# A longer planned distance between the loads and the sums of pooled keys and values in a fused attention and feed-forward kernel

## The chip, the cores and the metric

One NeuronCore of one Trainium2 chip runs the whole kernel. The metric is the device time of one execution in microseconds (us), given as the median of the runs; lower is better. The engines of the core are TensorE (PE in the profile; PEld is its weight load), VectorE (DVE), ScalarE (ACT), GpSimd (POOL) and SyncE (SP), which only issues transfers (DMAs) here. Each engine works through its own list of instructions in order.

## The reference

Attention over keys and values that are averaged in groups of eight tokens, and a feed-forward layer with softplus behind it:

```python
B, H, S, D = 8, 8, 576, 64          # q, k, v: (B, H, S, D), float32
k_p = k.reshape(B, H, 72, 8, D).mean(axis=3)
v_p = v.reshape(B, H, 72, 8, D).mean(axis=3)
scores = matmul(q, k_p.T) / sqrt(D)
attn = exp(scores - max) ; attn = attn / (sum(attn) + 1e-9)
x = matmul(attn, v_p)               # tokens x 512: (4608, 512)
h = x @ w_in                        # (512, 2048)
g = maximum(h, 0) + log1p(exp(-abs(h)))
out = g @ w_out                     # (2048, 512) -> (4608, 512)
```

## The kernel before

The 4608 tokens are cut into 18 chunks of 256 (`NCH`, numbered c = 0 to 17). A batch b has 576 tokens, so a new batch begins every 2.25 chunks, and a chunk has rows of one batch or of two. Products that need float32 accuracy are made of three fp32r products of a high and a low part.

**Chunks.** For each chunk, attention makes scores, probabilities and x, and the feed-forward layer then runs over eight pairs of rows of `w_in` and `w_out` (u = 0 to 7): the first product (line 678, 24 matmuls, output `h`), softplus on ScalarE (lines 686 and 700), sums and low parts on VectorE (lines 737 to 740, 707, 756), and the second product. For chunks 0 to 3 that is a plain product (lines 652 and 719), from chunk 4 on (`NF`) a product in 21 matmuls over sums of blocks (line 826, output `m`). During a steady chunk c the attention of chunk c + 1 is done in between: scores (line 490), then least values, differences, exponential, sums, transposes of the probabilities (line 556, `ptp`), and the product with the values (lines 597 and 604, `avp`).

**Two lists.** The order of all instructions is planned ahead by the class `Order` (lines 37 to 99). Every piece of work is an `op` with an engine, a cost, the ops that it comes after, the buffers (`Slot`) that it holds, and a lag: the time that must pass, in the plan, between its end and the start of an op on another engine that follows it (line 74). The planner runs through time and picks for an engine, among the ops that could start soon, the one with the highest rank; a rank is the longest way from the op to the end, costs and lags added (line 55), and some ops have a bonus (`first`) on top. What comes out is only an order on each engine. On the chip an instruction waits for semaphores that follow from the tiles that it reads and writes, not for planned times. The first list covers chunks 0 to 2 and the conversion of the weights; the steady list, from line 1375 on, covers the rest. Only the steady list has an object attribute `pause` (line 1382); in the first list `todo.pause` is the empty dictionary of the class.

**Keys and values.** `keys_values(b)` (line 1213) makes the ops of one batch, for b = 2 in the first list and for b = 3 to 7 in the steady list. Inside it `pooled` (line 1223) makes a pair: a load on SyncE into one of four staging buffers (`LD`, line 154), and a sum over eight tokens on VectorE (`tree`, line 227: two instructions on the staging buffer and one that writes the pooled tile). A batch has four such pairs for keys (line 263, one DMA each), two for values (line 275, two DMAs each) and one for the last eight rows of the values (line 287, four small DMAs, called the left rows here). In the plan, the load of a pair comes after the sum of the pair two places before it. After the four sums of keys, TensorE transposes them (line 234) and ScalarE writes `kT`; after the two of values, ScalarE writes `vs` (line 244); after the left rows come lines 299 and 251 and last line 253, which writes `vlo`, on which the first load of the next batch depends in the plan. `kT`, `vs` and `vlo` have two buffers each, by b % 2.

**What stands beside them.** On SyncE: `load_wi` (line 854), two DMAs of 512 KB for each pair u from chunk 4 on, as soon as TensorE has read the rows that they overwrite; the loads of q (line 333); the stores of the output (line 664); loads and stores of combined weights (lines 800 and 807) in chunks 3 and 4. On TensorE, inside the scores of a chunk: all but the last 1/8 of them go to two PSUM banks, the last eighth twice into one place, so that VectorE must copy the first of the two out (`keep`, line 504, `E<-x`) before TensorE may write the second (line 490, `x<-kT,qT`).

Of the kernel before, what the change touches and what calls it, by code (L numbers as in the profile page):

```python
# [30 lines left out]
class Order:  # L31
# [11 lines left out]
    def op(self, engine, cost, fn, after=(), slots=(), lag=None, rest=0, first=0, table=None):  # L43
        o = Op(engine, cost, fn, after, slots, self.HOP if lag is None else lag, len(self.ops))
        o.rest, o.first, o.table = rest, first + self.first, table
        for x in o.after:
            x.followers.append(o)
        for x in slots:
            x.users.append(o)
        self.ops.append(o)  # L50
        return o
# [54 lines left out]
def pooled_attention_softplus_ffn(  # L106
# [125 lines left out]
    def k_transposes(ps, kp):  # L232
        for m in range(HP):
            nc.tensor.transpose(out=ps[:, m * SP:(m + 1) * SP],
                                in_=kp[:, 2 * m:2 * m + 2].rearrange("p h d -> p (h d)"),
                                identity=ident[0:SP, 0:SP])

    def k_scaled(b, ps):

        nc.scalar.activation(out=kT[b % 2], in_=ps[:, 0:HP * SP].rearrange("p (m y) -> p m y", m=HP),  # L240
                             func=AF.Copy, scale=SCALE)

    def v_scaled(b, vp):
        nc.scalar.activation(out=vs[b % 2], in_=vp, func=AF.Copy, scale=1.0 / POOL)

    def left_part(b, i, lt):

        R, vx = 4 * KL, vlo[b % 2]
        lv = lt.rearrange("p a (m c) d -> p (a m) (c d)", c=2)
        if i < 2:  # L250
            nc.scalar.copy(out=vx[i * R:(i + 1) * R], in_=lv)
        else:
            nc.vector.tensor_tensor(out=vx[2 * R:3 * R], in0=lv, in1=vx[0:R].bitcast(F32),
                                    op=ALU.subtract)
# [51 lines left out]
    def spans(lo, hi):  # L306

        cut = sorted({lo, hi, *(x for x in range(0, NTOK, S) if lo < x < hi)})
        return [(x, y, x // S) for x, y in zip(cut, cut[1:])]
# [5 lines left out]
    def ones():  # L315
        x = one.tile([P, T, H, SP], F32, tag="E", name="ones").rearrange("p t h y -> p (t h y)")
        nc.vector.memset(x[:, 0:512], 1.0)
        return x
# [542 lines left out]
    todo = Order(kinds)  # L861
    op = todo.op
    ACT, DVE, PE, SYNC = (nc.scalar.engine, nc.vector.engine, nc.tensor.engine, nc.sync.engine)
    todo.begin, todo.table = {SYNC: 0.8, DVE: 0.8, PE: 0.8, ACT: 2.0}, "exp"

    def bank(s, name):
        if s.tile is None:
            s.tile = psum.tile([P, 512], F32, tag=s.name, name=name)
        return s.tile
# [3 lines left out]
    def act(n):  # L873
        return 0.14 + 0.00094 * n
# [338 lines left out]
    def keys_values(b, free_k=None, free_v=None):  # L1213
        x = kv(b)
        batches = lambda c: {y for _, _, y in spans(c * CT, (c + 1) * CT)}
        s_kp, s_vp, s_lt, s_vl = Slot("kp"), Slot("vp"), Slot("kp"), Slot("vp")

        old = [c for c in range(N1 + 1, NCH) if b - 2 in batches(c)]
        free_k = free_k or [o for c in old for o in score_done.get(c, ())]
        free_v = free_v or [o for c in old for o in av_done.get(c, ())]  # L1220
        ends = [v_ready[b - 1][-1] if b > 3 else None]

        def pooled(load, pool, time, slot, after=()):

            s = Slot("ld")
            o = op(SYNC, time, lambda: load(s), ends[-2:][:1], [s], lag=2.4)
            ends.append(op(DVE, 1.4, pool, [o, *after], [s, slot]))
            return ends[-1]

        sums_ = [pooled(lambda s, i=i: x["k_load"](i, s), lambda i=i: x["k_pool"](i), 1.2, s_kp)  # L1230
                 for i in range(HP)]
        s_t = Slot("bank")
        o = op(PE, 0.3, lambda: k_transposes(bank(s_t, "kT"), x["kp"][0]), [*sums_, *free_k],
               [s_t, s_kp], first=100)
        k_ready[b] = [op(ACT, act(288), lambda: k_scaled(b, s_t.tile), [o], [s_t])]
        sums_ = [pooled(lambda s, i=i: x["v_load"](i, s), lambda i=i: x["v_pool"](i), 1.2, s_vp)
                 for i in range(2)]
        v_ready[b] = [op(ACT, act(256), lambda: v_scaled(b, x["vp"][0]), [*sums_, *free_v], [s_vp])]
        o = pooled(lambda s: x["left_load"](s), x["left"], 1.0, s_vl, v_ready[b])
        o = op(DVE, 1.1, x["lasts"], [o, *k_ready[b]], [s_vl, s_lt])  # L1240
        parts = [op(ACT, 0.65, lambda i=i: left_part(b, i, x["st"]["lt"]), [o, *free_v], [s_lt])
                 for i in range(2)]
        v_ready[b].append(op(DVE, 0.7, lambda: left_part(b, 2, x["st"]["lt"]), parts, [s_lt]))
# [21 lines left out]
    o = op(DVE, 0.3, lambda: x_w.append(ones()), first=2000)  # L1265
# [113 lines left out]
    ends = {e: max(o.end for o in todo.ops if o.engine == e) for e in (ACT, DVE, PE, SYNC)}  # L1379
    todo = Order(kinds)  # L1380
    todo.begin = {e: max(0, t - ends[PE]) for e, t in ends.items()}
    todo.pause = {PE: 0.05, DVE: 0.5}
    op = todo.op
# [293 lines left out]
```

## Time and profile before

| | |
|---|---|
| median of 3 runs | 896.26 us (895.38 to 896.85) |
| the profiled execution | 896.75 us |
| its span, first to last instruction | 895.0 us |
| TensorE busy in the span | 873.6 us (98%) |
| VectorE, ScalarE busy | 643.9 us (72%), 418.1 us (47%) |
| mean granted TensorE clock | 0.989 of full speed |

The span is what the trace covers; 1.75 us of the execution lie around it. A share of busy time is a mean over stages, so what a single place costs is read from the waits and from stretches of the timeline. A releaser named beside an idle time is the event that came last ahead of the waiting instruction.

### The profile page before, as it was taken

The page shows a single profiled execution, that of the slowest core. Times are in us where ns is not written, and L with a number is a line of the kernel's source. Part 1 is how long each engine was busy: PE and PEld are TensorE (multiplying, and loading weights), DVE is VectorE, ACT ScalarE, POOL GpSimd, SP SyncE. Part 2 cuts the span into 40 slices and gives each one's busy share as a digit, 9 for nine tenths or more (in the row PEclk, how much of TensorE's full clock was granted, in tenths as well). Part 3 has the DMA queues.
Part 4 walks back from the last instruction along what each step waited for, and adds up shares of the span by engine and source line. Part 5 has one row for each costly group of instructions (what it writes and reads, how often), then busy time and mean ns, then how long its engine had stood idle before and what let it go on. Part 6 is the DMA issues. An engine that isn't in the chain of part 4 may idle for free.

```text
span 895.0 us, 20398 instructions
## 1 busy us (share of the span) xinstructions
PE 873.6 (98%) x8280; PEld 831.0 (93%) x8280; DVE 643.9 (72%) x1531; ACT 418.1 (47%) x851; POOL 2.4 (0%) x19
## 2 busy tenths in 40 slices
PE   6899999999999999998999999999999999999997
PEld 3688989888999999998999899999999999999997
DVE  6899998888867788685667756787676565656454
ACT  5854343355463636452554445353636353525332
POOL 1000000000000000000000000000000000000000
PEclk8999999999999999998999999999999999999999
DMA  8964535456897768595657756695757574646572
GB/s 251 306 223 168 189 127 168 160 180 198 275 293 245 242 224 290 186 278 174 219 198 264 227 202 209 215 279 199 230 190 234 183 231 168 226 162 212 188 242 89
DMA packets 107086, 191.12 MB, mean 214 GB/s; under 512 B 46065, under 2 KB 60401, under 8 KB 106993
## 3 DMA queue, kind: packets, MB, share of 16 engines
q1 hardware_dynamic: 106992, 189.82, 64.7%
q8 instruction: 65, 1.06, 0.5%
q14 instruction: 29, 0.23, 0.1%
HBM read 167.25 MB, written 22.54 MB: 212 GB/s over the span
## 4 chain that ended last, share of the span: by engine, by line
PE 91%; DMA 5%; DVE 2%; ACT 1%; issue 0%; SPq 0%; DVEq 0%; ACTq 0%
PE h L678 36%; PE m L826 29%; PE h L630 7%; PE acc L652 6%; DMA vst<-in_v_dram 3%; PE acc L719 3%; PE avp L597 1%; PE x L361 1%; PE ptp L556 1%; DMA q<-in_q_dram 1%; PE avp L604 1%; PE sc L490 1%; DMA kvst<-in_v_dram 1%; PE qTp L361 1%; PE vps L1081 1%; DVE vst L227 1%
## 5 line engine op out<-in xcount | busy, mean ns | idle before, releaser
L678 PE MATMUL h<-x,w 128*128 128x256 f32 x2880 | 349.2, 277 | 0.8 <-DVE x L614 0.8
L678 PEld LDWEIGHTS h<-x,w 128*128 128x128 f32 x2880 | 337.4, 188 | 1.7 <-PE acc L652 1.2
L686 ACT ACTIVATE g<-h 128x512 f32<-128x512 f32 x120 | 71.9, 599 | 250.5 <-PE h L678 250.3
L826 PE MATMUL m<-w,so 128*128 128x256 f32 x1344 | 173.6, 279 | 0.0
L826 PEld LDWEIGHTS m<-w,so 128*128 128x128 f32 x1344 | 163.6, 190 | 0.1
L826 PE MATMUL m<-w,gh 128*128 128x256 f32 x672 | 128.4, 281 | 0.0
L737 DVE TENSOR_TENSOR sf<-g 128x128 f32<-128x128 f32 x112 | 32.7, 292 | 127.3 <-ACT g L686 126.3
L826 PEld LDWEIGHTS m<-w,gh 128*128 128x128 f32 x672 | 102.4, 190 | 0.1
L751 ACT CAST so<-sf 128x512 fp32r<-128x512 f32 x112 | 69.7, 622 | 64.6 <-DVE sf L740 63.0
L756 DVE TENSOR_TENSOR so<-sf,so 128x512 fp32r<-128x512 f32 x112 | 77.3, 690 | 23.1 <-ACT so L751 23.1
L826 PE MATMUL m<-w,gl 128*128 128x256 f32 x336 | 93.6, 278 | 0.0
L630 PEld LDWEIGHTS h<-x,w 128*128 128x128 f32 x576 | 72.0, 189 | 3.8 <-DVE w L965 0.9
L630 PE MATMUL h<-x,w 128*128 128x256 f32 x576 | 73.4, 280 | 0.5 <-DVE w L965 0.5
L707 DVE TENSOR_TENSOR gl<-g,gh 128x384 fp32r<-128x384 f32 (+1 forms) x120 | 67.2, 560 | 2.9 <-PE acc L719 1.7
L826 PEld LDWEIGHTS m<-w,gl 128*128 128x128 f32 x336 | 63.7, 190 | 0.0
L635 ACT ACTIVATE g<-h 128x256 fp32r<-128x256 f32 x96 | 32.3, 383 | 67.2 <-PE h L630 47.8
L652 PE MATMUL acc<-w,g 128*128 128x512 f32 x192 | 60.9, 398 | 0.0
L700 ACT ACTIVATE gh<-h 128x384 fp32r<-128x384 f32 (+1 forms) x120 | 59.1, 493 | 0.0
L847 DVE TENSOR_TENSOR o<-o,m 128x256 f32<-128x256 f32 x98 | 39.7, 418 | 3.3 <-ACT o L839 0.4
L652 PEld LDWEIGHTS acc<-w,g 128*128 128x128 f32 x192 | 33.3, 188 | 5.4
L652 PE MATMUL acc<-w,gl 128*128 128x512 f32 x96 | 38.0, 396 | 0.0
L740 DVE TENSOR_TENSOR sf<-g,sf 128x128 f32<-128x128 f32 x112 | 32.7, 292 | 3.9
(207 smaller groups left out, 985.8 us busy)
## 6 DMA issues: line engine op xcount, KB each, us to landing
w<-wi SPq DMA_DIRECT2D x224, 512.0 KB
out_dram<-o SPq DMA_DIRECT2D x36, 256.0 KB
q<-in_q_dram SPq DMA_DIRECT2D x32, 256.0 KB
wst<-in_moe_w_in_dram SPq DMA_DIRECT2D x32, 256.0 KB
wst<-in_moe_w_out_dram SPq DMA_DIRECT2D x16, 512.0 KB
wi<-w SPq DMA_DIRECT2D x16, 512.0 KB
kst<-in_k_dram SPq DMA_DIRECT2D x24, 288.0 KB
vst<-in_v_dram SPq DMA_DIRECT2D x24, 256.0 KB
```

The costliest lines, as they stand in the source:

```text
L630: nc.tensor.matmul(out=ps[:, 0:CT], lhsT=row(w, kc), rhs=x[:, kc], start=first and kc == j == 0, stop=last and kc == KC - 1 and j == 2)
L652: nc.tensor.matmul(out=accs[c][t], lhsT=a[:, ts], rhs=w, start=f == 0 and j == 0, stop=f == FC - 1 and j == 2)
L678: nc.tensor.matmul(out=ps[:, k * CT:(k + 1) * CT], lhsT=row(w, kc), rhs=x_[c][i][:, kc], start=first and n == 0, stop=last and n == len(or ...
L686: nc.scalar.activation(out=g, in_=x.rearrange("p (b i) -> p b i", i=P), func=AF.Softplus)
L700: nc.scalar.activation(out=gh, in_=quarters(c, x.rearrange("p (b i) -> p b i", i=P)), func=AF.Softplus)
L707: nc.vector.tensor_tensor(out=gl, in0=quarters(c, g), in1=gh.bitcast(F32), op=ALU.subtract)
L737: tt(out=sf[:, 2], in0=g[:, 0], in1=g[:, 2], op=ALU.add)
L740: tt(out=sf[:, 3], in0=g[:, 3], in1=sf[:, 1], op=ALU.subtract)
L751: nc.scalar.copy(out=so[:, 0], in_=ss[c, u])
L756: nc.vector.tensor_tensor(out=so[:, 1], in0=sf, in1=so[:, 0].bitcast(F32), op=ALU.subtract)
L826: nc.tensor.matmul(out=ms[c][n], lhsT=x, rhs=y, start=u == 0 and j == 0 and n in (1, 6, 5, 4), stop=u == FP - 1 and j == 2 and n in (2, 7, ...
L847: nc.vector.tensor_tensor(out=o, in0=in0, in1=m[n], op=how)
```

## The change

In the steady list, and only there, the lag behind each load of keys or values is 9.0 in place of 2.4. The first list keeps 2.4. No instruction is added or taken away, no cost, buffer or wait of an op is changed; the planner is given another number and orders the steady list anew. The planned start of a sum is then at least 9.0 us after the planned end of its load's issue, and the rank of each load, and of everything that leads to one, rises with it.

```diff
@@ -1223,7 +1223,7 @@
         def pooled(load, pool, time, slot, after=()):
 
             s = Slot("ld")
-            o = op(SYNC, time, lambda: load(s), ends[-2:][:1], [s], lag=2.4)
+            o = op(SYNC, time, lambda: load(s), ends[-2:][:1], [s], lag=9.0 if todo.pause else 2.4)
             ends.append(op(DVE, 1.4, pool, [o, *after], [s, slot]))
             return ends[-1]
```

## Rows read from the trace of the kernel before

**Rows 1.** The page, part 4: the chain that ended last, by engine

```profile
PE 91%; DMA 5%; DVE 2%; ACT 1%; issue 0%; SPq 0%; DVEq 0%; ACTq 0%
```

**Rows 2.** Waits of TensorE, 380 to 620 us: waiter, releaser, total us, times, longest

```profile
PE x L490 <- DVE E L504: 5.9, 3, 3.3
```

**Rows 3.** Waits of VectorE, 180 to 640 us

```profile
DVE vst L227 <- DMA vst<-in_v_dram: 8.2, 5, 3.4
```

**Rows 4.** Timeline, first stop: start us, length, instruction, idle before and its releaser

```profile
401.06 2.14 SPq L275 DMA_DIRECT2D vst<-in_v_dram  x2
...
410.60 1.15 DVE L227 TENSOR_TENSOR vst<-vst 128x512 f32<-128x512 f32 x2 [3.37 <-DMA vst<-in_v_dram]
411.79 0.29 DVE L227 TENSOR_TENSOR vp<-vst 128x128 f32<-128x128 f32 x1
...
412.28 0.50 PE L490 MATMUL x<-kT,qT 64*64 64x72 f32 x4 [3.29 <-DVE E L504]
```

**Rows 5.** Timeline, second stop

```profile
499.32 1.25 SPq L275 DMA_DIRECT2D vst<-in_v_dram  x2
...
507.57 1.15 DVE L227 TENSOR_TENSOR vst<-vst 128x512 f32<-128x512 f32 x2 [2.50 <-DMA vst<-in_v_dram]
...
509.25 0.34 PE L490 MATMUL x<-kT,qT 64*64 64x72 f32 x4 [1.99 <-DVE E L504]
```

**Rows 6.** Timeline, third stop

```profile
595.68 1.34 SPq L275 DMA_DIRECT2D vst<-in_v_dram  x2
...
602.58 1.15 DVE L227 TENSOR_TENSOR vst<-vst 128x512 f32<-128x512 f32 x2 [1.12 <-DMA vst<-in_v_dram]
...
604.26 0.34 PE L490 MATMUL x<-kT,qT 64*64 64x72 f32 x4 [0.61 <-DVE E L504]
```

**Rows 7.** Stretches: length, busy us (instructions) by engine, PE clock, DMA share, GB/s

```profile
396.98:449.07 52.09, 48.80 (x464) 47.70 (x463) 34.85 (x90) 21.77 (x39) 0.00 (x0) 0.93 0.68 210
449.07:495.24 46.17, 46.17 (x469) 45.29 (x467) 32.29 (x86) 22.77 (x41) 0.00 (x0) 1.00 0.69 230
495.24:545.03 49.79, 47.80 (x465) 46.77 (x463) 33.48 (x87) 21.35 (x38) 0.00 (x0) 0.97 0.67 217
591.64:638.40 46.76, 46.15 (x464) 45.12 (x463) 34.77 (x90) 21.36 (x38) 0.00 (x0) 1.00 0.73 236
684.99:730.82 45.83, 45.83 (x464) 44.95 (x463) 28.22 (x75) 21.35 (x38) 0.00 (x0) 1.00 0.62 207
```

**Rows 8.** The stretch right behind the first stop

```profile
412.00:418.00 6.00, 5.72 (x29) 5.58 (x30) 5.18 (x15) 1.31 (x3) 0.00 (x0) 0.50 0.20 69
```

**Rows 9.** Timeline, batch 3: loads, sums and the products that need them

```profile
262.44 0.40 SPq L263 DMA_DIRECT2D kst<-in_k_dram  x1
...
263.31 1.34 SPq L275 DMA_DIRECT2D vst<-in_v_dram  x2
...
268.14 1.13 DVE L227 TENSOR_TENSOR kst<-kst 72x512 f32<-72x512 f32 x2
...
272.81 1.15 DVE L227 TENSOR_TENSOR vst<-vst 128x512 f32<-128x512 f32 x2 [0.48 <-DMA vst<-in_v_dram]
...
275.16 2.88 SPq L287 DMA_DIRECT2D lst<-in_v_dram  x4
...
294.59 1.12 DVE L227 TENSOR_TENSOR lst<-lst 32x512 f32<-32x512 f32 x2
...
306.54 0.68 DVE L253 TENSOR_TENSOR vlo<-lt,vlo 32x512 fp32r<-32x512 f32 x1
...
313.63 1.11 PE L597 MATMUL avp<-pT,vs 64*64 64x192 f32 x32
```

**Rows 10.** Timeline, batch 5: last step, and the product of chunk 11

```profile
470.08 0.68 DVE L253 TENSOR_TENSOR vlo<-lt,vlo 32x512 fp32r<-32x512 f32 x1
...
551.72 1.11 PE L597 MATMUL avp<-pT,vs 64*64 64x64 f32 x32
```

**Rows 11.** Waits of SyncE's queue, 180 to 640 us

```profile
SPq L854 <- PE h L678: 249.4, 68, 9.8
```

## The prediction

> **What bounds the kernel now.** I read the page's chain first. TensorE holds 91% of it, and transfers hold 5% [rows 1]. TensorE is the engine to fill, so the 5% is where something other than TensorE decided the time. The second view is the list of TensorE's waits. In the steady part there is one kind only: three times, 5.9 us in all, TensorE stands before the last eighth of the scores and waits for VectorE's copy of line 504 [rows 2]. That copy takes a fraction of a microsecond, so the question is why VectorE was late. VectorE's own waits answer it: five times, 8.2 us, it stood before a sum of values until the transfer into the staging buffer had landed [rows 3].
>
> The third view, the timeline, joins the two. The values' load at 401.06 lands just ahead of 410.60, where VectorE's sum starts after 3.37 us of idle. The copy that the scores need is listed behind that sum, and TensorE goes on at 412.28 after 3.29 us [rows 4]. The same happens at 507.57, with 1.99 us on TensorE [rows 5], and at 602.58, with 0.61 us [rows 6]. A list that is worked through in order makes VectorE's wait for data into TensorE's wait for an unrelated copy.
>
> The fourth view prices this: stretches from one transposition of probabilities (line 556) to the next, one chunk long each. With the same TensorE work (464 or 465 instructions) the undisturbed stretch takes 45.83 us, all of it busy; the three with a stop take 52.09, 49.79 and 46.76 us [rows 7]. More is lost than TensorE's idle time because the granted clock falls behind a stop: 0.50 of full speed, which is the 1.2 GHz level, in the 6 us behind the first [rows 8], and 0.97 on average over the stretch of the second [rows 7].
>
> **The change part by part.** The change adds and removes no instruction. It places the 35 sums of the steady list (five batches, seven each) by a load time of 9.0 us in place of 2.4, and it moves what hangs on them.
>
> *The waits it is to remove.* Surplus of the three stretches over the undisturbed one [rows 7]: 52.09 - 45.83 = 6.26 us, 49.79 - 45.83 = 3.96 us, 46.76 - 45.83 = 0.93 us, together 11.15 us. Of these 3.29 + 1.99 + 0.61 = 5.89 us are idle time [rows 4 to 6], and the other 5.26 us are matmuls at the lower clock or restarting.
>
> *Is 9.0 enough?* A planned sum now starts at least 1.2 (cost of the issue in the plan) + 9.0 = 10.2 us after the planned start of its load; before, it was 1.2 + 2.4 = 3.6 us. The trace says what a load needs, from its issue to the sum that waited for it: 410.60 - 401.06 = 9.54 us [rows 4], 507.57 - 499.32 = 8.25 us [rows 5], 602.58 - 595.68 = 6.90 us [rows 6], and 272.81 - 263.31 = 9.50 us in batch 3, where VectorE waited 0.48 us and TensorE not at all [rows 9]. All four lie under 10.2 us, by 0.66 us at the closest. So where the chip keeps the plan's distance, each of these sums finds its data. Where it doesn't, the rest of a wait falls on VectorE first. Bounds: nothing at best; at worst the loads are slower in their new places by as much as they already spread, 9.54 - 6.90 = 2.64 us, and a sum waits 2.64 - 0.66 = 1.98 us, about as long as TensorE's second stop, which cost 3.96 us with its clock. For three values' loads of the late batches that is 0 to 11.9 us. I take 0, since no load in the rows needs 10.2 us, and keep one such remainder in the range.
>
> Here a page speaks against the change. The Trainium skill, "DMA: Bandwidth & Descriptors", section "Anatomy of one DMA — SWDGE (gpsimd) path", fits a transfer at 2.0 us and its bytes at 436 GB/s, for another issuing path than SyncE's; two DMAs of 256 KB would then take an estimated 3.2 us, the old 3.6 us would be enough, and nothing would be gained. The trace differs: 6.9 to 9.5 us on a queue that is shared with the streamed weights, q and the output [rows 4 to 6].
>
> *The sums themselves.* Each is three instructions, 1.15 us for the two on the staging buffer and 0.29 us for the third [rows 4]. They stay the same 35 and only change neighbours. VectorE is busy 28.22 of 45.83 us in the stretch without them and 32.29 of 46.17 us in one with some of them in which TensorE is busy for the whole length [rows 7], so 14 to 17 us are free in a stretch and cover them. If a sum falls just ahead of the copy of line 504 without that cover, it costs at most its 1.15 + 0.29 = 1.44 us, and a faster order of the same list could gain as much. I take 0, by the stretch at 449.07.
>
> *The loads.* In the plan the load of a pair follows the sum two places before it, so a batch is four loads and sums in a row (two of keys, one of values, the left rows), each now at least 10.2 us apart. The minimum for a batch rises by up to 4 x 6.6 = 26.4 us. The rank of its first load rises by as much, so loads and sums are picked sooner, once they can be. Loads move past those of the streamed weights (line 854), which stand in SyncE's queue for 249.4 us in 68 waits until TensorE has read the rows [rows 11]. What is listed behind such a wait, loads of keys and values too, starts late by it, and its sum was planned without that. In the other direction a keys' or values' load ahead of a weights' load delays it by the 0.40 to 1.34 us of the issue [rows 9], plus the time of its bytes. TensorE never waited for a weights' load in the rows [rows 2], so some cover is there. Bounds: 0 and 1.34 us for each crossing; I take 0.
>
> *Who needs the results.* Only batch 3 is close. Its `vlo` is done at 306.54 + 0.68 = 307.22, and the product of chunk 6 starts at 313.63: 6.41 us of room [rows 9]. Batch 5 has 551.72 - 470.76 = 80.96 us [rows 10]. For batch 3 the 26.4 us are mostly there already: the values' pair goes from 9.50 to 10.2 us, the fourth keys' pair from 268.14 - 262.44 = 5.70 to 10.2 us, and the left rows had 294.59 - 275.16 = 19.43 us, more than they now must have [rows 9]. A delay of 4.5 + 0.7 = 5.2 us ahead of the left rows fits into the 19.43 - 10.0 = 9.4 us that they can give up (their issue is planned at 1.0). I take 0.
>
> *What is late next.* With the three stops gone, the stretches are bound as the one at 684.99 is, by TensorE at 45.83 of 45.83 us busy and a clock of 1.00 [rows 7]. Nothing else ends late behind it.
>
> *The sum.* The profiled execution is 896.75 us, with a span of 895.0 us and 1.75 us around it; the median is 0.49 us lower, 896.26 us. 896.75 - 11.15 = 885.60 us for an execution like the profiled one, and 896.26 - 11.15 = 885.1 us for the median.
>
> **The rivals.**
>
> *One stop stays.* A sum behind a late SyncE issue, or a load slower than 10.2 us, leaves a stop like one of the three. The plan is drawn anew, so it need not be at one of the old places. For: the margin at 401.06 is only 0.66 us, and the weights' waits in SyncE's queue move real issues away from planned ones [rows 4, 11]. Against: a sum planned later is also a sum that VectorE reaches later, and in a new place the copy of line 504 need not stand right behind it. With the second stop's price it gives 885.1 + 3.96 = 889.1 us, with the first one's 885.1 + 6.26 = 891.4 us.
>
> *The change doesn't do what it says.* If SyncE's issues slip with the sums, because the loads go behind the same waits for TensorE, the distance on the chip stays what it was, stops of about the same size stand elsewhere, and the time is about 896.3 us. For: 249.4 us of such waits [rows 11]. Against: the waits are for TensorE, which runs to plan outside the stops (rows 7: 45.83 and 46.17 us, all busy).
>
> *Slower: batch 3 comes late.* If the extra 26.4 us of the chain aren't absorbed by the gaps that batch 3 already has, `vlo` is ready at 307.22 + 26.4 = 333.6, the product of chunk 6 waits 26.4 - 6.41 = 20.0 us, and the first product of chunk 6 behind it, since the feed-forward work of the chunk before it runs out. With the gain of 11.15 us elsewhere that is 896.26 + 20.0 - 11.15 = 905.1 us. It begins to cost at 6.41 us of delay, and makes the kernel slower at 6.41 + 11.15 = 17.6 us. Against it: the gaps of rows 9 leave about 5 us of delay ahead of the left rows, and those had more than that to spare. For it: batch 3's loads share SyncE with chunk 4's additional loads of combined weights, and what the planner does there isn't to be read from the trace of before.
>
> **How the numbers follow.** All three stops gone, 883.5 to 887.5 us: 0.64. One stop left, to 893 us: 0.17. About the old time: 0.08. Slower: 0.11. The likeliest is 885.1 us. The range goes from 884.0 us (one microsecond under the forecast, for what a new order of the same list may give) to 893.0 us, which takes in a stop of the first one's size and a remainder of up to 1.6 us; the other two cases, 0.19, lie outside. A measurement of this kernel can tell some 0.2%, 1.8 us, from no change: below 894.5 us counts as faster (0.81), above 898.1 us as slower (0.11), between them as the same (0.08).
>
> **What would show it.** Right: TensorE's list of waits has no line 490 behind line 504 in the steady part; VectorE's wait for the values' transfers falls from 8.2 us to under 1 us; the stretches from one line 556 to the next are 45.8 to 46.7 us long throughout; the mean clock rises from 0.989; sums start 10 us or more behind their loads. Wrong: a wait of VectorE on line 227 that is followed by one of TensorE, wherever it is; weights' loads or batch 3's keys and values (lines 234, 244, 253) as releasers of TensorE; sums as close behind the issues as before. The prediction fails if the new order of the steady list brings a stop that the old one hid.

## The result, and the profile after

The changed kernel takes 886.64 us (median of 6 runs, 886.15 to 888.70) beside 895.87 us for the kernel before (median of 6, 894.36 to 897.92): a ratio of 0.9900, with an interval of 0.9884 to 0.9916. That is 9.2 us less. The profiled execution has a span of 884.4 us where the one of before had 895.0 us, and a mean granted clock of 0.995 where it was 0.989.

TensorE's waits from 180 to 880 us, all of them (waiter, releaser, total us, times, longest). The three waits at line 490 [rows 2] are gone:

```profile
PE h L678 <- DVE x L614: 0.8, 1, 0.8
PE x L563 <- DVE pe L547: 0.2, 1, 0.2
```

The first of the two stands in the kernel before as well, with the same 0.8 us; the second is new. The place of the first stop on the changed kernel's timeline (start us, length, instruction, idle before and its releaser):

```profile
408.74 0.23 DVE L504 COPY E<-x 128x72 f32<-128x72 f32 x1 [1.35 <-PE x L490]
...
411.57 0.23 DVE L504 COPY E<-x 128x72 f32<-128x72 f32 x1
...
418.12 1.14 DVE L227 TENSOR_TENSOR kst<-kst 72x512 f32<-72x512 f32 x2
```

No sum stands ahead of the copies now, and VectorE waits for TensorE there, the right way round; in rows 4 TensorE waited 3.29 us for VectorE. The sum behind them is one of keys: the whole batch has moved.

The stretches from one transposition of probabilities to the next, to be laid beside rows 7 (length, busy us and instructions by engine, clock, DMA share, GB/s). The first three are the chunks that had the stops, the fourth is the undisturbed one:

```profile
397.56:443.39 45.83, 45.83 (x464) 44.95 (x463) 34.88 (x92) 22.41 (x40) 0.00 (x0) 1.00 0.72 240
489.55:535.39 45.84, 45.84 (x465) 44.96 (x463) 34.75 (x90) 21.35 (x38) 0.00 (x0) 1.00 0.75 249
581.99:627.82 45.83, 45.83 (x464) 44.95 (x463) 34.70 (x90) 21.35 (x38) 0.00 (x0) 1.00 0.72 236
674.40:720.23 45.83, 45.83 (x464) 44.95 (x463) 28.24 (x75) 21.35 (x38) 0.00 (x0) 1.00 0.62 208
```

52.09, 49.79 and 46.76 us have become 45.83, 45.84 and 45.83 us. All 11.15 us of the three stops are back, at a clock of 1.00. But some of it is lost again earlier. Three stretches in a row, first of the changed kernel:

```profile
257.32:306.99 49.67, 49.48 (x493) 48.23 (x491) 33.64 (x88) 22.60 (x42) 0.00 (x0) 1.00 0.80 253
306.99:350.53 43.54, 43.54 (x460) 43.06 (x459) 32.04 (x85) 21.80 (x39) 0.00 (x0) 1.00 0.70 231
350.53:397.56 47.03, 47.03 (x468) 46.15 (x467) 34.79 (x90) 21.94 (x40) 0.00 (x0) 1.00 0.72 235
```

and the same three of the kernel before:

```profile
258.39:304.56 46.17, 46.17 (x469) 45.28 (x467) 34.91 (x90) 22.08 (x40) 0.00 (x0) 1.00 0.82 253
304.56:350.82 46.26, 46.26 (x484) 45.78 (x483) 36.13 (x95) 22.58 (x40) 0.00 (x0) 1.00 0.78 258
350.82:396.98 46.16, 46.16 (x468) 45.28 (x467) 34.98 (x92) 23.10 (x42) 0.00 (x0) 1.00 0.71 228
```

The first two belong together, because one block of 24 matmuls has moved from the second into the first: 49.67 + 43.54 = 93.21 us beside 46.17 + 46.26 = 92.43 us, 0.78 us more. The third is 47.03 - 46.16 = 0.87 us longer with the same 468 instructions, and no idle time in either. So the change itself brings 11.15 - 0.78 - 0.87 = 9.50 us in this pair of executions, close to the 9.2 us of the medians; the rest of the spans' difference, 1.07 us, lies ahead of 258.39 and 257.32 us. It is there already at 215.31 and 214.24 us, ahead of the first instruction that the two kernels have in another order (near 238 us), so the change didn't make it; the profiled executions of all the kernels here reach this place between 213.4 and 216.1 us. The lengths 49.67 and 43.54 us come again, within 0.06 us, in the two runs below that are built on the changed kernel, so the 0.78 us are of the order and not of one execution.

What the 0.78 us are, on the changed kernel's timeline of batch 3, to be laid beside rows 9:

```profile
276.33 1.13 DVE L227 TENSOR_TENSOR kst<-kst 72x512 f32<-72x512 f32 x2
...
281.15 1.03 PE L490 MATMUL sc<-kT,qT 64*64 64x72 f32 x52
...
299.16 1.35 DVE L528 TENSOR_REDUCE sm<-E 128x16 f32<-128x1152 f32 x1 [1.37 <-ACT E L325]
...
300.93 0.63 DVE L756 TENSOR_TENSOR so<-sf,so 128x512 fp32r<-128x512 f32 x1
...
301.61 1.24 PEld L826 LDWEIGHTS m<-w,so 128*128 128x128 f32 x10 [0.23 <-DVE so L756]
...
306.39 0.38 PE L563 MATMUL x<-ident,pe 128*64 128x128 f32 x2 [0.15 <-DVE pe L547]
...
316.06 0.68 DVE L253 TENSOR_TENSOR vlo<-lt,vlo 32x512 fp32r<-32x512 f32 x1
...
318.44 1.11 PE L597 MATMUL avp<-pT,vs 64*64 64x192 f32 x32
```

The fourth sum of keys starts at 276.33 in place of 268.14, the scores of chunk 6 come later with it, and so does all that follows from them on VectorE and ScalarE. Two short stops of TensorE come of it. At 299.16 VectorE's sums of the exponentials start after 1.37 us of waiting for ScalarE; the low parts of line 756 are listed behind them, and TensorE's weight load waits 0.23 us for these (a wait of PEld, so not in the list above). Then the probabilities reach TensorE a block later than before and just too late: line 563 waits 0.15 us. The block of 21 matmuls that starts at 300.50 and the block of 24 behind it, with the idle time and a slower pace between the two stops, take 306.39 - 300.50 = 5.89 us in place of 2.38 + 2.72 = 5.10 us, which is all of the loss. The first of these stops is of the kind that the change removes: an unrelated wait stands in VectorE's list ahead of something that TensorE needs. `vlo` is done at 316.74, 1.70 us ahead of the product that needs it, in place of 6.41 us.

What the 0.87 us are: in the chain of the changed kernel (start us, length, piece) the blocks grow longer behind the transposition of batch 4's keys, and stay so until the next transposition of probabilities:

```profile
370.42 2.72 PE h L678 x24
373.14 0.26 PE kT L234 x4
373.40 2.52 PE m L826 x21
375.92 2.83 PE h L678 x24
378.75 2.47 PE m L826 x21
381.22 2.83 PE h L678 x24
```

24 matmuls take 2.83 us and 21 take 2.47 us where they took 2.72 and 2.38 us, 4% more, without idle time and at a granted clock of 1.00. In the kernel before that transposition stood at another place, two blocks ahead of scores that ended the run.

### The profile page after: what moved, and what is told of

Its sections match the earlier page's. It is cut to its first block, busy times and chain, and to the rows that moved or that the text cites. A ratio compares the mean times of both kernels' runs of the same rounds, so it can differ in the third digit from the quotient of the medians.

```text
span 884.4 us, 20405 instructions
## 1 busy us (share of the span) xinstructions
PE 869.4 (98%) x8280; PEld 827.2 (94%) x8280; DVE 643.6 (73%) x1531; ACT 417.6 (47%) x851; POOL 2.4 (0%) x19
## 4 chain that ended last, share of the span: by engine, by line
PE 92%; DVE 3%; DMA 2%; ACT 1%; issue 1%; SPq 0%; DVEq 0%; ACTq 0%
PE h L678 37%; PE m L826 30%; PE h L630 6%; PE acc L652 6%; PE acc L719 3%; PE avp L597 2%; PE x L361 2%; PE avp L604 1%; PE sc L490 1%; PE ptp L556 1%; DMA vst<-in_v_dram 1%; ACT E L412 1%; DMA q<-in_q_dram 1%; PE qTp L361 1%; PE vps L1081 1%
## 5 line engine op out<-in xcount | busy, mean ns | idle before, releaser
L826 PE MATMUL m<-w,so 128*128 128x256 f32 x1344 | 171.8, 277 | 0.0
L826 PEld LDWEIGHTS m<-w,so 128*128 128x128 f32 x1344 | 161.5, 188 | 0.3 <-DVE so L756 0.2
L614 DVE TENSOR_TENSOR x<-avp,x 128x512 fp32r<-128x512 f32 x36 | 23.4, 686 | 17.4 <-ACT x L611 17.3
```

The lines of the kernel that those rows point to most:

```text
L826: nc.tensor.matmul(out=ms[c][n], lhsT=x, rhs=y, start=u == 0 and j == 0 and n in (1, 6, 5, 4), stop=u == FP - 1 and j == 2 and n in (2, 7, ...
```

## The experiments

All stretches named below run from one transposition of probabilities to the next. The kernel before varied more beside these runs than beside the first ones (medians of 898 to 900 us on their chips), so the ratios to it carry that; what a run shows is read from its own stretches and waits. From 215 us on most stretches of the same order agree between runs to 0.01 us; the exceptions, all in batch 3's chunk or the one behind it, are named where they occur.

**Only the three sums moved.** The order of the kernel before, with three sums of values listed behind the second copy of line 504:

```diff
+        order = todo.run()
+        for y in (5, 6, 7):            # moved[y]: the sum at the stop, the copy of batch 5's values
+            pool, scaled = moved[y]
+            i = order.index(pool)
+            to = next(n for n in range(i, len(order)) if order[n] in copied)   # keep(1)
+            j = order.index(scaled)
+            order.insert(to, order.pop(i))
+            if j <= to:
+                order.insert(to, order.pop(j - 1))
-        for o in todo.run():
+        for o in order:
```

> The kernel before, with its order of instructions kept on TensorE and SyncE, and on VectorE but for three sums: the sums of values at the three stops (batches 5, 6 and 7) are listed behind the second of the two copies of line 504, eight instructions later each; the scaled copy of batch 5's values moves with its sum on ScalarE. Loads, distances and everything else stay. Theory A (TensorE stopped only because the copy was listed behind a sum whose data was late): the three waits of TensorE go, and the stretches that took 52.09, 49.79 and 46.76 us take 45.8: 896 - 11.2 = 885 us. Rival B (the late transfers themselves cost it, through what else hangs on these sums or through a full queue): the sums still wait for the same data, other waits take the place of the old ones, and the time stays above 891 us.

Measured: 886.58 us (883.91 to 890.29), ratio 0.9882 (0.9841 to 0.9923). TensorE has no wait at line 490, and the three stretches:

```profile
397.85:443.68 45.83, 45.83 (x465) 44.95 (x463) 34.76 (x90) 21.77 (x39) 0.00 (x0) 1.00 0.74 237
489.84:535.68 45.84, 45.84 (x465) 44.96 (x463) 33.59 (x87) 21.35 (x38) 0.00 (x0) 1.00 0.75 235
582.28:628.11 45.83, 45.83 (x464) 44.95 (x463) 34.80 (x90) 21.34 (x38) 0.00 (x0) 1.00 0.80 243
```

Three sums, each eight instructions later in VectorE's list, give what the new order of the whole list gave. SyncE issues the transfers in the order of before; theory A holds against rival B. The profiled execution has slower blocks too, from 275.7 to 319.1 us, though TensorE's list is that of the kernel before; they lengthen two stretches to 47.40 and 46.55 us, 1.52 us over those of before. Ahead of them VectorE waited 1.4 us for batch 3's keys and 0.6 us for its values, with a copy of line 504 behind.

**The longer lag for batches 5 to 7 only.**

```diff
-lag=9.0 if todo.pause else 2.4)
+lag=9.0 if todo.pause and b > 4 else 2.4)
```

> The lag of 9.0 for batches 5 to 7 only, 2.4 for 3 and 4. Theory A: all three stops were in batches 5 to 7, so they go as with the change; and the surplus that the changed kernel has between 257 and 398 us (0.8 us where batch 3's scores came later, 0.9 us behind batch 4's transposition of keys) does not arise: 1.7 us under the changed kernel, about 885 us. Rival (that surplus is chance of another kind, or batches 3 and 4 gave part of the gain): the same as the changed kernel, 886.6 us, or slower.

Measured: 885.13 us (882.86 to 886.72). The three chunks are at 45.83 us, and the three stretches from 257.76 us on are back at the lengths of before:

```profile
257.76:303.93 46.17, 46.17 (x469) 45.29 (x467) 34.94 (x90) 22.06 (x40) 0.00 (x0) 1.00 0.80 252
303.93:350.19 46.26, 46.26 (x484) 45.78 (x483) 36.15 (x95) 22.57 (x40) 0.00 (x0) 1.00 0.77 257
350.19:396.35 46.16, 46.16 (x468) 45.27 (x467) 33.68 (x89) 23.09 (x42) 0.00 (x0) 1.00 0.69 226
```

Both losses of the change, 0.78 and 0.87 us, come from the longer lag of batches 3 and 4, which had no stop to lose.

**Full transpositions added behind small products.** In the changed kernel, one more matmul behind each transposition of keys and one behind the scores of the last chunk:

```diff
+        if todo.pause:
+            nc.tensor.transpose(out=ps[:, 512 - P:512], in_=ident, identity=ident)
...
             turn()
+            if c == NCH - 1:
+                nc.tensor.transpose(out=r.tile[:, 512 - P:512], in_=ident, identity=ident)
```

> The changed kernel with six more transpositions on TensorE, each of the 128x128 identity into unused columns of a bank: one behind each of the five transpositions of keys in the steady list, one behind the scores of the last chunk. Theory: the blocks of 24 and 21 matmuls that take 2.83 and 2.47 us in place of 2.72 and 2.38 us (373 to 397 us, 779 to 813 us) follow a small product directly, and a transposition of full size behind it brings them back: 1.7 us less, 0.7 us of it paid for six transpositions of 0.11 us, about 885.6 us, and no block of 24 over 2.76 us there. Rival (the slower blocks come from something else that runs at that time, a transfer or another engine): the blocks stay at 2.83 and 2.47 us and the time rises by up to 0.7 us.

Measured: 885.95 us (884.26 to 887.43). Half of the theory held. The last chunk's stretch, of the changed kernel and of this one:

```profile
766.49:813.21 46.72, 46.72 (x461) 45.84 (x459) 28.10 (x75) 21.07 (x37) 0.00 (x0) 1.00 0.55 192
```

```profile
766.01:811.50 45.49, 45.49 (x461) 44.60 (x460) 28.02 (x75) 21.08 (x37) 0.00 (x0) 1.00 0.56 195
```

The slower blocks there are gone, 1.23 us for one matmul of 0.11 us. Behind batch 4's keys the same matmul does nothing: the blocks stay at 2.83 and 2.47 us, and the stretch takes 47.09 us.

**Both edits on the kernel before.** The three sums moved and the six transpositions added, the diffs of the first and the third run together, with the lag of 2.4.

> The kernel before with the three sums moved as in the run that only moves them, and with the six added transpositions. Theory: the 11.2 us of the three stops and the 0.9 us of slower blocks in the last chunk's stretch, less up to 0.7 us for the six transpositions: about 884.5 us, faster than the changed kernel by some 2 us. Rival as for the two edits alone: 885 us or more.

Measured: 885.06 us (883.28 to 888.70), span 881.6 us. In the stretches the gains add as expected: 45.83 or 45.84 us three times, 45.49 us in the last chunk, 46.22 us where a transposition was added. The median, 0.6 us over the 884.5 us expected, doesn't by itself exclude the rival's 885 us.

**Other lags: 4.0, 6.5 and 12.0 in place of 9.0.**

```diff
-lag=9.0 if todo.pause else 2.4)
+lag=4.0 if todo.pause else 2.4)        # and 6.5, 12.0
```

> The changed kernel with a lag of 4.0 in place of 9.0, so that a sum is planned at least 1.2 + 4.0 = 5.2 us behind its load, less than any of the four loads needed that a sum waited for (6.90 to 9.54 us). Theory A (the distance has to reach what a load needs): the order changes, but stops stay, three waits of TensorE at line 490 of a similar size, 893 to 897 us. Rival C (any new order of the list loses the three stops, the distance itself matters little): no stops, 885 to 887 us.

Measured: 884.87 us (884.70 to 885.57). Theory A in this form falls: not one stop is left. The timeline shows why (the second load of batch 5's values, the first copy, the sum):

```profile
401.04 2.52 SPq L275 DMA_DIRECT2D vst<-in_v_dram  x2
...
408.14 0.23 DVE L504 COPY E<-x 128x72 f32<-128x72 f32 x1 [1.35 <-PE x L490]
...
417.52 1.14 DVE L227 TENSOR_TENSOR vst<-vst 128x512 f32<-128x512 f32 x2
```

Planned at 5.2 us behind its load or later, the sum starts 16.5 us behind it. It missed the place ahead of the copies, and the next one was behind them and behind the least values and differences of the scores. All stretches from 258 us on, but for those of the three stops, have the lengths of before to 0.01 us, so this lag has the whole gain and none of the losses in this execution.

> The changed kernel with a lag of 6.5: planned at least 7.7 us behind the load, over the 6.90 us of the third stop's load and under the 8.25 and 9.54 us of the other two. Theory A: the remainders 8.25 - 7.7 and 9.54 - 7.7 are up to 1.8 us on VectorE, and TensorE waits for at most that where its copy is behind such a sum: 885 to 891 us, between the other two lags. Rival C: as with 9.0, 886.6 us.

Measured: 884.41 us (883.25 to 886.35), no stop. Again not what theory A said, and the lengths of the stretches are again those of the lag of 4.0. From 250 us on VectorE waits for no transfer of keys or values at all, where it still waited 0.5 us with the lag of 4.0.

> The changed kernel with a lag of 12.0. Theory A: the stops are gone already at 9.0, nothing more is to be had there; batch 3's chain of four loads gets up to 4 x 3 = 12 us longer, the product of chunk 6 had 1.7 us of room left in the changed kernel, so the stretches from 257 us on lose more than the 0.8 us that they lost with 9.0: 887 to 897 us. Rival (batch 3 has more gaps than its rows show): 886.6 us as with 9.0, with the same stretches.

Measured: 886.89 us (886.57 to 888.93), no stop. Batch 3 did not get worse: the two stretches that took 93.21 us take 49.13 + 43.54 = 92.67 us. What this lag loses is slower blocks behind the transpositions of keys of two batches, in stretches of 47.24 and 47.68 us where the lag of 4.0 has 46.16 and 46.60 us, and 0.24 us of batch 3's 0.78 us, where line 563 alone still comes late.

**A lag of 3.0**, the smallest step tried:

```diff
-lag=9.0 if todo.pause else 2.4)
+lag=3.0 if todo.pause else 2.4)
```

> The changed kernel with a lag of 3.0, by which TensorE and SyncE have the same order as in the kernel before and only the order on VectorE and ScalarE differs. A sum is planned at least 4.2 us behind its load in place of 3.6. Theory D, formed after the lag of 4.0 (the distance decides only whether a sum still fits into the free place ahead of the scores' copies; once it misses it, its next place is 16 us behind the load): either the sum still fits and the three stops stay, 893 to 897 us, or it misses and they are gone, 884 to 886 us, and nothing between for one stop. Theory A in its first form (stops shrink as the distance grows): each stop 0.6 us shorter, about 893 us.

Measured: 885.03 us (884.38 to 886.15). The place of the first stop, then VectorE's waits for values from 380 to 620 us:

```profile
400.06 1.89 SPq L275 DMA_DIRECT2D vst<-in_v_dram  x2
...
407.16 0.23 DVE L504 COPY E<-x 128x72 f32<-128x72 f32 x1 [1.35 <-PE x L490]
...
409.01 1.15 DVE L227 TENSOR_TENSOR vst<-vst 128x512 f32<-128x512 f32 x2 [1.61 <-DMA vst<-in_v_dram]
...
412.71 0.23 DVE L504 COPY E<-x 128x72 f32<-128x72 f32 x1
```

```profile
DVE vst L227 <- DMA vst<-in_v_dram: 3.5, 3, 1.6
```

The sum has moved by a single place, from ahead of the first copy to behind it. VectorE still waits for the values in all three chunks, 3.5 us, and TensorE doesn't: the stretches are 45.83, 45.84 and 45.83 us. Only the first copy is what TensorE needs soon. Theory D fits, with a correction: the sum didn't have to go far behind its load. SyncE and TensorE have the order of the kernel before here, so neither a moved load nor a moved matmul did it. One stretch is longer, 47.11 us from 256.45 us on, where batch 3's keys came late to VectorE by 2.8 us in this execution and TensorE's transposition of them waited 0.7 us.

**The transposition of batch 4's keys moved.** In the changed kernel, five blocks later on TensorE:

```diff
+        order = todo.run()
+        i, j = (order.index(o) for o in turned[4])      # the transposition, the copy of its result
+        to = [n for n in range(i + 1, len(order)) if order[n].engine == PE][7]
+        order.insert(to, order.pop(j))
+        order.insert(to - 1, order.pop(i))
-        for o in todo.run():
+        for o in order:
```

> The changed kernel with one step moved: the transposition of batch 4's keys on TensorE, and the copy of its result on ScalarE, some ten microseconds later, into the middle of the same run of blocks. Theory (the blocks of 24 and 21 matmuls slow from 2.72 and 2.38 to 2.83 and 2.47 us because that small product stands directly ahead of a long run of them): the slow blocks now begin behind the transposition, near 384 us, and the stretch that took 47.03 us takes 46.4 to 46.7 us. Rival (they begin at 373 us for another reason, the sums of batch 4's keys and values on VectorE or their loads, which keep their places): slow from 373 us on as before, 47.0 us.

Measured, one execution: 885.43 us. The slower blocks begin behind it again, at 385.75 us, and the stretch takes 46.54 us, as the theory said:

```profile
380.39 2.72 PE h L678 x24
383.11 2.38 PE m L826 x21
385.49 0.26 PE kT L234 x4
385.75 2.88 PE h L678 x24
388.62 2.47 PE m L826 x21
391.10 2.83 PE h L678 x24
```

**Versions meant to beat both.** The lag of 9.0 for batches 5 to 7, or the lag of 4.0 for all, each with one added transposition behind the last scores:

```diff
-lag=9.0 if todo.pause else 2.4)
+lag=9.0 if todo.pause and b > 4 else 2.4)     # the second kernel: lag=4.0 if todo.pause else 2.4
...
             turn()
+            if c == NCH - 1:
+                nc.tensor.transpose(out=r.tile[:, 512 - P:512], in_=ident, identity=ident)
```

> The lag of 9.0 for batches 5 to 7 only, and one added transposition of the identity behind the scores of the last chunk. Theory: the two gains add, 1.7 us under the changed kernel from batches 3 and 4 and 1.2 us from the last chunk's stretch (46.72 to 45.49 us where the transposition was added before): a span of about 882 us and 884 us, the lowest of all. Rival: the stretch of the last chunk stays at 46.7 us, 885.1 us as without it.

Measured: 884.75 us (882.56 to 888.42), span 881.5 us, the last chunk's stretch 45.49 us. The span and the stretches are as expected; the median lies between theory and rival and decides nothing.

> A lag of 4.0 for all five batches, and one added transposition of the identity behind the scores of the last chunk. The two gains are in different stretches: all stretches as with the lag of 4.0, and the last chunk's 45.49 in place of 46.71 us: a span of 882 to 883 us, about 883.7 us. Rival: no sum of gains, 884.9 us as with the lag alone.

Measured: 883.54 us (882.36 to 884.43), ratio 0.9825 (0.9794 to 0.9856), span 881.9 us. It has the lowest median of all the kernels; it was not run side by side with the changed kernel. Its stretches are those of the lag of 4.0 but for the last chunk's 45.49 us and one of 46.66 in place of 46.16 us, ahead of 303.79 us. There, in batch 3's chunk, the lag of 4.0 keeps a sum of values ahead of the copy of line 504, as the kernel before does. In this execution its data came late, and TensorE's weight load waited:

```profile
273.97 1.15 DVE L227 TENSOR_TENSOR vst<-vst 128x512 f32<-128x512 f32 x2 [1.52 <-DMA vst<-in_v_dram]
...
276.76 0.23 DVE L504 COPY E<-x 128x72 f32<-128x72 f32 x1
...
277.04 0.19 PEld L490 LDWEIGHTS x<-kT,qT 64*64 64x64 f32 x4 [0.24 <-DVE E L504]
```

So the lags of 3.0 and 4.0 leave a fourth place of the kind that stops TensorE, which cost nothing in one execution and some 0.5 us in another.

## Why the prediction was right, and where it was off

**What bounds the kernel: right.** Three stops of TensorE behind a copy that was listed behind a late sum. The run that moved only three sums shows the cause alone, and the price of 11.15 us was right to 0.01 us for each stretch of this pair of executions, the slow clock behind the stops included.

**Is 9.0 enough: true, but not the step that decides.** The changed kernel's sums start 12.8 us or more behind their loads, past the 9.54 us that the slowest of the four needed, and VectorE no longer waits for any load of keys or values behind 250 us. The bound itself was too low: with the lag of 4.0 a load of batch 3's values took 10.9 us until the sum that waited for it could start, and 11.9 us with the added transposition, both over the 10.2 us that were thought enough. But the prediction took the arrival of the data for the condition, and the planned distance for the real one. The lags of 3.0, 4.0 and 6.5 fall short of it by that sum and lose the stops as well. What decides is whether the sum stands ahead of the first copy or behind it. VectorE's list has few places that a sum fits in, so a small change of the lag moves it by a whole place, and the late sums behind the copy cost TensorE nothing in the three chunks.

**Who needs the results: right in kind, off in size.** Batch 3 was named as the only close one, and priced at 0 with 5.2 us of delay in front of the left rows. The fourth sum of keys alone came 276.33 - 268.14 = 8.19 us later, where 4.5 us were worked out; it starts 14.97 us behind its load, not at the 10.2 us that the lag allows, since a sum takes the next place in the list. `vlo` came 316.74 - 307.22 = 9.52 us later. By the prediction that costs from 6.41 us on, but the product that needs `vlo` came 4.81 us later too and kept 1.70 us of room. The 0.78 us were lost on a path that the prediction did not price: the scores, the exponentials and the probabilities of chunk 6, by way of VectorE's low parts (line 756) and of line 563.

**What is moved: one thing was left out.** The prediction followed sums on VectorE and loads on SyncE, and took 0 for their new neighbours. It did not follow the transposition of keys, which goes behind the fourth sum, to TensorE. Batch 4's landed at the head of a long run of blocks, which then ran 4% slower: 0.87 us. That the place caused it is shown for this batch alone; why it does is open (see the last section).

**The sum.** 885.1 us was forecast, 886.64 us came. The two omitted terms, 0.78 + 0.87 = 1.65 us, are about the 1.5 us of difference. That they agree so closely is in part luck, since the profiled executions differ by more than that ahead of any work that was moved (213.4 to 216.1 us at the same place). None of the rivals took place: no stop of line 490 is left, the change does what it says, and batch 3's delay of 9.52 us stayed under the 17.6 us that it would have taken to make the kernel slower.

**The signs.** Line 490 is gone from TensorE's waits, VectorE's wait for the values fell from 8.2 us to nothing, the clock rose to 0.995, and all sums of the steady list start more than 10 us behind their loads. One sign failed: the stretches are not 45.8 to 46.7 us long throughout, but 49.67, 43.54 and 47.03 us where the losses are, the first two also because a block moved between them. And the new order did bring stops that the old one hid, though small ones: 0.23 and 0.15 us.

## What to carry to other kernels

Where an engine works through a list in order, ask of each instruction that waits for a transfer what is listed behind it and who waits for that; putting the urgent one ahead is enough, and the data may go on being late. A planner's time constant moves work by whole places, so a value a little above the old one can give all that a large one gives; but it also leaves other places where a late load can still stop an engine in some executions, as batch 3's did for 0.5 to 0.9 us with the lags of 4.0 and 3.0. The large one removed these waits and moved work that had nothing to gain; the one between, 6.5, had neither loss in its trace. Follow what moves through every engine that it ends on: the losses here showed on TensorE, not where the constant was.

## What the runs showed of the hardware that was not expected

Blocks of TensorE's matmuls (128x128 weights, 256 columns) have two speeds with no idle time and a granted clock of 1.00 in both: 2.72 us for 24 and 2.38 us for 21, or 2.83 and 2.47 us. In the changed kernel the slower one began directly behind the four transpositions of 72 rows of batch 4's keys, began behind them again when they were moved, and lasted until the next transposition of probabilities. But a small product ahead of a long run of blocks is not enough. With the lag of 12.0 four batches have their transposition in such a place, with the same block ahead of it and the same blocks behind; batches 4 and 6 are followed by slower blocks, batches 5 and 7 are not. Batch 4's and batch 5's, from the chain of that run:

```profile
367.48 0.25 PE kT L234 x4
...
370.26 2.83 PE h L678 x24
```

```profile
460.55 0.26 PE kT L234 x4
...
463.25 2.72 PE h L678 x24
```

The slower speed also began behind the last chunk's scores in every kernel without the added transposition, this one's stretch being 46.71 or 46.72 us, and one full transposition of 0.11 us kept it away there (45.49 or 45.50 us) in all four kernels that had it, but did not behind the keys. In the changed kernel it began once more at 301.61 us, behind the weight load's wait of 0.23 us, and in the run that moved only the sums behind scores that a transposition of q followed. Nor does it always end at a transposition of probabilities: in that last case it went on past the one near 305 us until 319.1 us. What sets it is open.
